# A limit of six loads in flight on one queue, and a warm-up cut into smaller products

## Chip, core and metric

The kernel runs on one core of a Trainium2 chip. The core has five engines that run side by side: TensorE (PE, matrix products; its weight loads are shown apart as PEld), VectorE (DVE), ScalarE (ACT), GpSimd (POOL) and SyncE (SP), which here only issues DMA transfers. Engines wait for one another, and for transfers, through semaphores. Sixteen DMA engines move data between the device memory (HBM) and the core's on-chip memory; a transfer is cut into pieces over all sixteen, and it has landed when the last of them is done.

The metric is the device time of one execution in microseconds (us), as a median over several runs.

## What is computed

The reference is an attention block without a softmax over keys, followed by a mixture-of-depths block. Shapes: 8 batches, 8 heads, 576 rows, head size 64; model width 512, hidden width 1024, capacity 128.

```python
q_s = exp(q - max(q, -1));  q_s /= sum(q_s, -1)      # over the head's 64 columns
k_s = exp(k - max(k, 2));   k_s /= sum(k_s, 2)       # over the 576 rows
kv  = einsum('bhsd,bhse->bhde', k_s, v)              # 64 x 64 for each head
x   = einsum('bhsd,bhde->bhse', q_s, kv)             # then heads side by side: B, S, 512

scores = einsum('bsd,d->bs', x, w_gate)
out = x.copy()
for b in range(B):
    top = the 128 rows of batch b with the largest scores
    h   = maximum(x[b, top] @ w1, 0)
    out[b, top] = x[b, top] + sigmoid(scores[b, top])[:, None] * (h @ w2)
```

## The kernel before, in words

Work is cut into 16 units; a unit is four heads of one batch, so two units make a batch. The program is written with a manual schedule: each engine runs its instructions in the order in which the code emits them, and an instruction that waits holds up everything behind it on its own engine.

For a unit, the loads bring k, v and q in two transfers each: for k and v one of 256 KB and one of 320 KB, for q two of 288 KB (three late units, 11, 13 and 15, take their q in four transfers of 144 KB with another layout, line 122). ACT takes the exponential of k (`k_exp`, line 249) and of q (`q_exp`, line 257); v is copied into a tile with a column of ones (`v_copy`, `v_copy_part`, lines 275 and 280, on DVE, POOL or ACT); TensorE forms kv (`kv_mm`, line 311, or `kv_mm_parts`, line 299, for unit 1), transposes q (`q_t`, lines 340 and 347) and multiplies the two (`x_mm`, line 375); DVE scales the result (`x_scale`, line 393), and SyncE stores it in two transfers (`x_store`, line 404). From the second unit of a batch on, scores are ranked (`compare`, line 443), the 128 best rows are gathered from the output by POOL (`fetch`, line 493), run through the two weight matrices (line 555 and line 564 for single batches, lines 648 and 704 for pairs of batches), and scattered back (line 573). The gathers read rows that the stores have written, so they wait for those stores.

Each of q, k and v has three buffers (`LD = 3`), so a load for unit u also waits until the buffer's user of unit u - 3 is done.

All loads are issued by SyncE, except one half of unit 0's k and the row of gate weights, which ACT issues. The function `load` (line 112) holds the issue calls for k, v and q, `load_w1` (line 154) four transfers of 512 KB, and `load_w2` (line 161) two of 1024 KB. The order at the start is: k, v, q of unit 0; q, k, v of unit 1; k of unit 2; then, behind a memset that DVE runs for the buffer, v and q of unit 2; w1; unit 3; unit 4; w2. The first stores, of unit 2, come after w2. Units 0 and 1 are stored much later (line 1104). After the start, each unit brings six loads and two stores in turn.

TensorE's first instructions are a warm-up: 12 products of 512 columns of ones (line 174), whose result nobody reads. Behind them come four products that spread the gate weights over partitions (line 860), one filler product (`fill`, line 854), and then kv of unit 0 (line 311), which needs the exponential of k from ACT and the copy of v from DVE.

`general` (line 777) is a fallback for inputs outside a range that the program checks at its end. It issues loads through the same functions and is not run for these inputs.

Of the kernel before, what the change touches and what calls it, by code (L numbers as in the profile page):

```python
# [17 lines left out]
def kernel(  # L18
# [23 lines left out]
    nc = tc.nc  # L42
    B, H, S, D = q.shape
    DM, F = moe_w1.shape
    P = 128
    R = 5
    N2 = R - 1
    T = R + N2
# [4 lines left out]
    SD = S * D  # L53
# [7 lines left out]
    NV = 5  # L61
    TURNED = frozenset((11, 13, 15))
    HC = 32
    WARM = 12
    assert S == 64 * T and D == 64 and DM == H * D and DM == 512 and H % 4 == 0
    assert 1 < capacity < S and KF == 8 and NQ == 2
    assert B * S <= 32 * 256
# [14 lines left out]
    def bank(tag, bufs):  # L82
        return ps.tile([P, 512], F32, tag=tag, name=tag, bufs=bufs)
# [9 lines left out]
    def place(b):  # L93
        return (b - 1) % B
# [4 lines left out]
    def rows_of(b, upward):  # L99
# [4 lines left out]


    LD = 3
    raw = {w: [const.tile([P, 2, T, D] if w == "q" else [P, 4, R, D], F32, name=f"{w}{n}") for n in range(LD)]
           for w in "qkv"}

    by_vector = TURNED  # L110

    def load(u, which, queues=(nc.sync, nc.sync)):
        b, qd = units[u]
        for what in which:
            src = {"q": q, "k": k, "v": v}[what]
            t = raw[what][u % LD]
            first = src[place(b), 4 * qd].offset
            if what == "q" and u in by_vector:

                for g in range(4):  # L120
                    i, c = divmod(g, 2)
                    nc.sync.dma_start(
                        out=t.rearrange("p h r d -> p (h r d)")[HC * g:HC * (g + 1)],
                        in_=bass.AP(tensor=src.tensor, offset=first + 2 * i * SD + HC * c,
                                    ap=[[T * D, HC], [D, T], [SD // 2, 4], [1, HC]]))
                continue
            if what == "q":
                for h in range(2):
                    queues[h].dma_start(out=t[:, h].rearrange("p r d -> p (r d)"),
                                        in_=bass.AP(tensor=src.tensor, offset=first + 2 * h * SD,  # L130
                                                    ap=[[T * D, P], [1, T * D]]))
                continue
            for n, rows in ((1, N2), (0, R)):
                queues[n].dma_start(
                    out=t[n::2, :, :rows].rearrange("p h r d -> p h (r d)"),
                    in_=bass.AP(tensor=src.tensor, offset=first + n * R * D,
                                ap=[[T * D, 64], [SD, 4], [1, rows * D]]))

    ctx.enter_context(tc.manual_schedule())
    for what in "kv":  # L140
# [7 lines left out]
                                               ap=[[DM, 1], [1, DM]]))  # L148
    w1 = const.tile([P, KD, F], F32, name="w1")
    w2 = const.tile([P, KF, DM], F32, name="w2")  # L150
# [3 lines left out]
    def load_w1(half):  # L154

        c = slice(half * F // 2, (half + 1) * F // 2)
        for d in range(0, KD, 2):
            nc.sync.dma_start(out=w1[:, d:d + 2, c],
                              in_=moe_w1[d * P:(d + 2) * P, c].rearrange("(d p) f -> p d f", p=P))

    def load_w2(n):
        half = KF // 2
        nc.sync.dma_start(out=w2[:, n * half:(n + 1) * half],
                          in_=moe_w2[n * half * P:(n + 1) * half * P].rearrange("(f p) d -> p f d", p=P))

    ones_b = const.tile([P, 4 * P], BF16, name="ones_b")
    nc.vector.memset(ones_b, 1.0)
    w_ps = bank("tp", 2)  # L170
    ones_f = const.tile([1, D], F32, name="ones_f")
    nc.vector.memset(ones_f, 1.0)
    for n in range(WARM):
        nc.tensor.matmul(out=w_ps, lhsT=ones_b[:, :P], rhs=ones_b, start=True, stop=True)
    warm = const.tile([P, 1], F32, name="warm")
    nc.scalar.activation(out=warm, in_=ones_b[:, :1], func=AF.Exp)
    ident = const.tile([P, P], F32, name="ident")
# [20 lines left out]
    for n in range(2):  # L198
        t = const.tile([P, 2, C], F32, name=f"kv_w{n}")
# [47 lines left out]
    def k_exp(u):  # L247
        ke = at.tile([P, 4, R, D], F32, tag="ke", name="ke", bufs=1)
        nc.scalar.activation(out=ke, in_=raw["k"][u % LD], func=AF.Exp)  # L249
        st["ke", u] = ke  # L250

    def q_exp(u, c):
        if c == 0:
            st["qe", u] = at.tile([P, T, 2, D], F32, tag="qe", name="qe", bufs=1)
        r0, r1 = ROWS[c]
        qr = raw["q"][u % LD].rearrange("p i r d -> p r i d")
        nc.scalar.activation(out=st["qe", u][:, r0:r1], in_=qr[:, r0:r1], func=AF.Exp)  # L257

    def q_exp_turned(u):
        qe = st["qe", u] = at.tile([P, T, 2, D], F32, tag="qe", name="qe", bufs=1)  # L260
        nc.scalar.activation(out=qe.rearrange("p r a t -> p (r a t)"),
                             in_=raw["q"][u % LD].rearrange("p h r d -> p (h r d)"), func=AF.Exp)

# [9 lines left out]
    def v_copy(u, engine=nc.vector):  # L273
        copy = engine.copy if engine is nc.scalar else engine.tensor_copy
        copy(out=v_ones[:, :, :, :D], in_=raw["v"][u % LD])  # L275

# [25 lines left out]
    def kv_mm(u, pairs=range(2)):  # L302

        ke, vo = st["ke", u], v_ones
        if 0 in pairs:
            st["kv", u] = bank("tp", 2)[:, :2 * (D + 1)].rearrange("p (i c) -> p i c", i=2)
        kv = st["kv", u]
        for i in pairs:
            for r in range(R):
                for h in range(2):  # L310
                    nc.tensor.matmul(out=kv[part(h), i], lhsT=ke[:, 2 * h + i, r], rhs=vo[:, 2 * h + i, r],  # L311
                                     start=(r == 0), stop=(r == N2))

    def kv_out(u):

        qd = units[u][1]
        kv = st.pop(("kv", u))
        kw = kv_w[u % 2]
        nc.vector.reciprocal(out=krec[:, u], in_=kv[:, :, D])
        nc.vector.tensor_mul(kw[:, :, :D], kv[:, :, :D], krec[:, u].to_broadcast([P, 2, D]))  # L320
        prod = at.tile([P, 2, D], F32, tag="prod", name="prod")
        for i in range(2):
            nc.vector.scalar_tensor_tensor(prod[:, i], kv[:, i, :D], krec[:, u, i:i + 1], wg[:, qd, i],
                                           op0=OP.mult, op1=OP.mult, accum_out=kw[:, i, D + 1:])
# [29 lines left out]
    def x_mm(u, a, wide=False):  # L354


        qT = st["qT", u] if a == 0 else st.pop(("qT", u))
        x = st["x", u, a] = ps.tile([P, 2, 512], F32, tag="x", name="x", bufs=2)
        kw = kv_w[u % 2]
        for r in range(R):  # L360
            for i, c in QUARTERS:
                if r == N2 and c:

                    nc.tensor.matmul(out=x[part(c), i, r * C:(r + 1) * C], lhsT=ones_b[part(i), :D],
                                     rhs=ones_b[part(i), :C], start=True, stop=True)
                    continue
                if wide and c:
                    continue
                both = wide and r < N2
                to = x[:, i] if both else x[part(c), i]  # L370
                if u in by_vector:
                    lhsT = qT[part(i), R * c + r, a]
                else:
                    lhsT = qT[part(i), a, r].rearrange("p c t -> p (c t)") if both else qT[part(i), a, r, c]
                nc.tensor.matmul(out=to[:, r * C:(r + 1) * C], lhsT=lhsT, rhs=kw[part(i), a], start=True, stop=True)  # L375
# [20 lines left out]
    def x_out(u):  # L396
        x_sums(u)
        x_scale(u, 0)
        x_scale(u, 1)
# [375 lines left out]
        nc.vector.tensor_sub(t, t, qm.to_broadcast([P, 2 * T, D]))  # L775

    def general():
        nonlocal by_vector
        by_vector = frozenset()
        for half in range(2):  # L780
            load_w1(half)
            load_w2(half)
        for b in range(B):
            for u in (NQ * b, NQ * b + 1):
                load(u, "kvq")
                shift(u)
                k_exp(u)
                q_exp(u, 0)
                q_exp(u, 1)
                v_copy(u)  # L790
                kv_mm(u)
                kv_out(u)
                q_t(u, 0)
                q_t(u, 1)
                for i in range(2):
                    x_mm(u, i)
                x_out(u)
                x_store(u)
            score(b, 0)
            score_parts(b)  # L800
            score_row(b, 1.0)
            for r in range(R):
                compare_exact(b, r)
            for step in (hits, find, fetch, gate, gated, turn):
                step(b)
            for f in range(KF):
                mlp1(b, f)
            for f in range(KF):
                mlp2(b, f)
            finish(b)  # L810
# [48 lines left out]
    for h in range(2):  # L859
        nc.tensor.matmul(out=g_ps[part(h), :4 * D], lhsT=ones_f,  # L860
                         rhs=w_row.rearrange("o (n i x) -> o i n x", i=2, x=2 * D)[:, h], start=True, stop=True)
# [11 lines left out]
    q_t(0, 1)  # L873
    load(2, "vq")
    load_w1(0)
    load_w1(1)
    q_exp(1, 0)
    q_exp(1, 1)
# [123 lines left out]
    for s in range(FIRST, SETTLED):  # L1002
        odd = s % 2 == 1
        here = s // 2 if odd else s // 2 - 1
        first = s == FIRST + 1
# [200 lines left out]
```

## Time and profile before

| what | us |
|---|---|
| median of 3 runs | 196.93 |
| the three runs | 196.46, 196.93, 198.37 |
| the profiled execution | 197.7 |
| its span, first to last instruction | 195.8 |
| TensorE busy in the span | 184.2 |

The profile is of one execution, which took 197.7 us; the span of its own instructions is 195.8 us, and the remaining 1.9 us lie around it. Times in the views count from the start of the span. A row of the chain of waits has a start, a length and what was under way; the time order of an engine has a start, a length, the engine (with a q where it is only its sequencer that issues a transfer), the line, the operation, the tiles as out<-in, and how many were merged into the row; brackets hold the idle time before it and what ended it.

### The profile page before, as it was taken

The page shows a single profiled execution, that of the slowest core. Times are in us where ns is not written, and L with a number is a line of the kernel's source. Part 1 is how long each engine was busy: PE and PEld are TensorE (multiplying, and loading weights), DVE is VectorE, ACT ScalarE, POOL GpSimd, SP SyncE. Part 2 cuts the span into 40 slices and gives each one's busy share as a digit, 9 for nine tenths or more (in the row PEclk, how much of TensorE's full clock was granted, in tenths as well). Part 3 has the DMA queues.
Part 4 walks back from the last instruction along what each step waited for, and adds up shares of the span by engine and source line. Part 5 has one row for each costly group of instructions (what it writes and reads, how often), then busy time and mean ns, then how long its engine had stood idle before and what let it go on. Part 6 is the DMA issues. An engine that isn't in the chain of part 4 may idle for free.

```text
span 195.8 us, 7049 instructions
## 1 busy us (share of the span) xinstructions
PE 184.2 (94%) x2927; PEld 156.0 (80%) x2927; DVE 130.4 (67%) x429; ACT 99.7 (51%) x160; POOL 72.7 (37%) x131
## 2 busy tenths in 40 slices
PE   5798899999999999999999999999999999999990
PEld 2466699894679996769999888899998889898860
DVE  6377966494669749928978989489959955444010
ACT  3474625658199759938675759365423133312100
POOL 8013551100860392099682312242314354701230
PEclk9999999999999999999999999999999999999997
DMA  5999999999999999989999799989451514010011
GB/s 153 364 365 378 378 368 364 328 388 352 341 379 374 336 314 363 308 248 152 312 325 320 130 317 330 273 160 257 158 121 57 121 38 149 32 54 5 3 56 63
DMA packets 48361, 46.67 MB, mean 238 GB/s; under 512 B 16321, under 2 KB 41921, under 8 KB 48322
## 3 DMA queue, kind: packets, MB, share of 16 engines
q1 hardware_dynamic: 46768, 41.62, 67.4%
q0 software_dynamic: 1280, 4.20, 6.7%
q8 instruction: 25, 0.41, 0.9%
q10 hardware_dynamic: 274, 0.33, 0.5%
q14 instruction: 14, 0.11, 0.2%
HBM read 34.61 MB, written 11.53 MB: 236 GB/s over the span
## 4 chain that ended last, share of the span: by engine, by line
PE 85%; DVE 6%; DMA 3%; issue 1%; ACT 1%; POOL 1%; POOLq 0%; DVEq 0%
PE mm L704 19%; PE mm L648 18%; PE tp L311 10%; PE x L375 10%; PE mm L555 8%; PE mm L564 8%; PE x L347 4%; DMA v<-in_v_dram 3%; PE mm L509 2%; PE tp L432 2%; PE x L530 2%; DVE xs L393 1%; DVE v_ones L280 0%; PE tp L468 0%; DVE v_ones L275 0%
## 5 line engine op out<-in xcount | busy, mean ns | idle before, releaser
L443 DVE SCALAR_TENSOR_TENSOR junk<-srow,s,stairs 128x576 bf16<-128x576 f32 x40 | 33.4, 834 | 1.5 <-ACT srow L435 0.8
L393 DVE TENSOR_TENSOR xs<-x,qrec 128x640 f32<-128x640 f32 x32 | 25.2, 815 | 0.0
L375 PE MATMUL x<-kv_w,qT 64*64 64x66 f32 x1152 | 23.2, 222 | 1.2 <-issue 0.5
L375 PEld LDWEIGHTS x<-kv_w,qT 64*64 64x64 f32 x1152 | 20.7, 134 | 4.5 <-issue 2.1
L352 ACT COPY qT<-x 128x512 f32<-128x512 f32 (+1 forms) x24 | 14.3, 643 | 17.1 <-PE x L347 16.6
L311 PE MATMUL tp<-v_ones,ke 128*64 128x65 f32 x600 | 21.6, 224 | 1.4 <-DVE v_ones L275 1.1
L704 PE MATMUL mm<-w,hT 128*128 128x256 f32 x96 | 22.2, 379 | 0.0
L249 ACT ACTIVATE ke<-k 128x1280 f32<-128x1280 f32 x16 | 20.4, 1274 | 3.4 <-issue 1.4
L311 PEld LDWEIGHTS tp<-v_ones,ke 128*64 128x64 f32 x600 | 19.2, 137 | 3.6 <-issue 1.9
L493 POOL DMA_INDIRECT xr<-out_dram,idx x8 | 8.1, 1018 | 36.3 <-DVE no L486 9.8
L704 PEld LDWEIGHTS mm<-w,hT 128*128 128x128 f32 x96 | 17.8, 190 | 2.2
L257 ACT ACTIVATE qe<-q 128x640 f32<-128x640 f32 (+1 forms) x26 | 16.4, 683 | 5.7 <-DMA q<-in_q_dram 3.0
L704 PE MATMUL mm<-tw,hT 128*128 128x256 f32 (+1 forms) x80 | 17.6, 363 | 0.0
L648 PE MATMUL mm<-xT,w 128*128 128x128 f32 x144 | 17.5, 276 | 0.0
L275 ACT COPY v_ones<-v 128x1280 f32<-128x1280 f32 x12 | 15.1, 1258 | 3.8 <-PE tp L311 2.5
L648 PEld LDWEIGHTS mm<-xT,w 128*128 128x128 f32 x144 | 16.8, 192 | 0.1
L555 PE MATMUL mm<-xT,w 128*128 128x128 f32 x128 | 16.7, 281 | 0.0
L713 POOL TENSOR_TENSOR o<-o,xr 128x256 f32<-128x256 f32 x9 | 6.8, 757 | 23.6 <-ACT o L712 23.6
L564 PE MATMUL mm<-w,hT 128*128 128x512 f32 x32 | 15.6, 611 | 0.0
L555 PEld LDWEIGHTS mm<-xT,w 128*128 128x128 f32 x128 | 15.0, 191 | 0.5
L704 PEld LDWEIGHTS mm<-tw,hT 128*128 128x128 f32 x80 | 13.8, 190 | 2.0 <-DVE o L717 0.4
L386 DVE RECIPROCAL qrec<-x 128x10 f32<-128x10 f32 x32 | 7.0, 217 | 12.6 <-PE x L375 12.2
(162 smaller groups left out, 311.2 us busy)
## 6 DMA issues: line engine op xcount, KB each, us to landing
q<-in_q_dram SPq DMA_DIRECT2D x26, 288.0 KB, 5.7
v<-in_v_dram SPq DMA_DIRECT2D x16, 320.0 KB, 5.4
out_dram<-xs SPq DMA_DIRECT2D x16, 320.0 KB, 5.6
k<-in_k_dram SPq DMA_DIRECT2D x15, 320.0 KB
k<-in_k_dram SPq DMA_DIRECT2D x16, 256.0 KB, 5.9
v<-in_v_dram SPq DMA_DIRECT2D x16, 256.0 KB
out_dram<-xs SPq DMA_DIRECT2D x16, 256.0 KB, 4.8
w<-in_moe_w_dram SPq DMA_DIRECT2D x4, 512.0 KB, 8.2
```

The source lines that it names most:

```text
L249: nc.scalar.activation(out=ke, in_=raw["k"][u % LD], func=AF.Exp)
L257: nc.scalar.activation(out=st["qe", u][:, r0:r1], in_=qr[:, r0:r1], func=AF.Exp)
L275: copy(out=v_ones[:, :, :, :D], in_=raw["v"][u % LD])
L311: nc.tensor.matmul(out=kv[part(h), i], lhsT=ke[:, 2 * h + i, r], rhs=vo[:, 2 * h + i, r], start=(r == 0), stop=(r == N2))
L352: nc.scalar.copy(out=to, in_=src)
L375: nc.tensor.matmul(out=to[:, r * C:(r + 1) * C], lhsT=lhsT, rhs=kw[part(i), a], start=True, stop=True)
L393: nc.vector.tensor_mul(xs[b][:, :, qd, :, a].rearrange("p r i d -> p i r d"), x[:, :, :, :D], rec.to_broadcast([P, 2, R, D]))
L443: nc.vector.scalar_tensor_tensor(junk, st["srow", b], st["s", b][:, r:r + 1], not_before[r], op0=OP.subtract, op1=OP.is_ge, accum_out=st[" ...
L555: nc.tensor.matmul(out=h_ps[:, f % HT * m:(f % HT + 1) * m], lhsT=w1[:, d, f * P:(f + 1) * P], rhs=xT[:, d, :m], start=(d == 0), stop=(d = ...
L564: nc.tensor.matmul(out=st["y", b][:m], lhsT=st["hT", b][:, f // HT, f % HT, :m], rhs=w2[:, f], start=(f == 0), stop=(f == KF - 1))
L648: nc.tensor.matmul(out=out_ps[:, f * m:(f + 1) * m], lhsT=w[:, k, f * P:(f + 1) * P], rhs=x()[:, k], start=first and f == 0 and k == 0, st ...
L704: nc.tensor.matmul(out=ps_of[to][:m, c:c + step], lhsT=st["hT", a][:, n, f, :m], rhs=w[:, f, c:c + step], start=first and f == 0, stop=f = ...
```

## The change

Two things are changed. A function `paced` is put around every issue of a load of q, k, v, w1 and w2. It keeps the names of the loads in the order of issue, and from the seventh on it makes each wait until the load six places ahead has landed. Stores and the gate weights are not counted and get no wait. ACT's half of unit 0's k is counted, as the second load. In the fallback the list is switched off.

The warm-up has 22 products of 280 columns in place of 12 of 512.

```diff
-    WARM = 12
+    WARM = 22
...
     LD = 3
+    AHEAD = 6
+    transfers = []
+
+    def paced(inst):
+
+        ins = inst.ins
+        if transfers is not None:
+            transfers.append(ins.name)
+            if len(transfers) > AHEAD:
+                tc.add_manual_dep(ins, transfers[-1 - AHEAD], mybir.DependencyInfo(
+                    mybir.DependencyClass.Sync, mybir.DependencyReason.DATA))
...
             for n, rows in ((1, N2), (0, R)):
-                queues[n].dma_start(
+                paced(queues[n].dma_start(
                     out=t[n::2, :, :rows].rearrange("p h r d -> p h (r d)"),
                     in_=bass.AP(tensor=src.tensor, offset=first + n * R * D,
-                                ap=[[T * D, 64], [SD, 4], [1, rows * D]]))
+                                ap=[[T * D, 64], [SD, 4], [1, rows * D]])))
...
     for n in range(WARM):
-        nc.tensor.matmul(out=w_ps, lhsT=ones_b[:, :P], rhs=ones_b, start=True, stop=True)
+        nc.tensor.matmul(out=w_ps[:, :280], lhsT=ones_b[:, :P], rhs=ones_b[:, :280], start=True, stop=True)
...
     def general():
-        nonlocal by_vector
+        nonlocal by_vector, transfers
         by_vector = frozenset()
+        transfers = None
```

The calls for q (both layouts), w1 and w2 are wrapped in the same way as that for k and v.

More of the change, by code (lines that the diff above doesn't have):

```diff
@@ L121, in load @@
                     i, c = divmod(g, 2)
-                    nc.sync.dma_start(
+                    paced(nc.sync.dma_start(
                         out=t.rearrange("p h r d -> p (h r d)")[HC * g:HC * (g + 1)],
                         in_=bass.AP(tensor=src.tensor, offset=first + 2 * i * SD + HC * c,
-                                    ap=[[T * D, HC], [D, T], [SD // 2, 4], [1, HC]]))
+                                    ap=[[T * D, HC], [D, T], [SD // 2, 4], [1, HC]])))
                 continue
@@ L128, in load @@
                 for h in range(2):
-                    queues[h].dma_start(out=t[:, h].rearrange("p r d -> p (r d)"),
-                                        in_=bass.AP(tensor=src.tensor, offset=first + 2 * h * SD,
-                                                    ap=[[T * D, P], [1, T * D]]))
+                    paced(queues[h].dma_start(out=t[:, h].rearrange("p r d -> p (r d)"),
+                                              in_=bass.AP(tensor=src.tensor, offset=first + 2 * h * SD,
+                                                          ap=[[T * D, P], [1, T * D]])))
                 continue
             for n, rows in ((1, N2), (0, R)):
-                queues[n].dma_start(
+                paced(queues[n].dma_start(
                     out=t[n::2, :, :rows].rearrange("p h r d -> p h (r d)"),
                     in_=bass.AP(tensor=src.tensor, offset=first + n * R * D,
-                                ap=[[T * D, 64], [SD, 4], [1, rows * D]]))
+                                ap=[[T * D, 64], [SD, 4], [1, rows * D]])))
     ctx.enter_context(tc.manual_schedule())
@@ L157, in load_w1 @@
         for d in range(0, KD, 2):
-            nc.sync.dma_start(out=w1[:, d:d + 2, c],
-                              in_=moe_w1[d * P:(d + 2) * P, c].rearrange("(d p) f -> p d f", p=P))
+            paced(nc.sync.dma_start(out=w1[:, d:d + 2, c],
+                                    in_=moe_w1[d * P:(d + 2) * P, c].rearrange("(d p) f -> p d f", p=P)))
     def load_w2(n):
         half = KF // 2
-        nc.sync.dma_start(out=w2[:, n * half:(n + 1) * half],
-                          in_=moe_w2[n * half * P:(n + 1) * half * P].rearrange("(f p) d -> p f d", p=P))
+        paced(nc.sync.dma_start(out=w2[:, n * half:(n + 1) * half],
+                                in_=moe_w2[n * half * P:(n + 1) * half * P].rearrange("(f p) d -> p f d", p=P)))
     ones_b = const.tile([P, 4 * P], BF16, name="ones_b")
```

## The prediction

> **What bounds the kernel now.** I read the page first, then the engines' busy time by stretches, the chain of waits, and last SyncE's own order of time.
>
> ```profile
> span 195.8 us, 7049 instructions
> PE 184.2 (94%) x2927; PEld 156.0 (80%) x2927; DVE 130.4 (67%) x429; ACT 99.7 (51%) x160; POOL 72.7 (37%) x131
> ...
> DMA  5999999999999999989999799989451514010011
> ...
> 8.50:24.00 15.50, 13.36 (x328) 10.75 (x329) 11.62 (x39) 9.71 (x15) 4.91 (x12) 1.00 1.06 375
> 24.00:190.00 166.00, 165.02 (x2581) 143.44 (x2581) 113.89 (x363) 87.20 (x142) 63.16 (x105) 1.00 0.75 232
> ```
>
> The first three lines are the page, the last two the stretches (length, then the busy time of PE, weight load, DVE, ACT and POOL, the clock, the DMA share and GB/s). From 24 to 190 us TensorE is busy for 165.02 of 166.00 us: later than that, a load that lands sooner brings nothing, and one that lands later costs nothing until its slack is used up. Time can move in the first 24 us, where TensorE idles for 15.50 - 13.36 = 2.14 us after 8.50, and before that. In the same time the DMA engines are full, at 375 GB/s, and stay so for most of the first half of the span.
>
> ```profile
> 2.32 5.13 DMA v<-in_v_dram
> ...
> 13.32 0.47 DVE xs L393
> ...
> 13.97 0.97 DVE v_ones L280
> ...
> 18.02 0.73 POOL v_ones L280
> ...
> 18.80 0.80 PE tp L311 x20
> ```
>
> This is the head of the chain of waits (start, length, what). Unit 0 starts when the second half of its v lands, at 2.32 + 5.13 = 7.45 us. Unit 1's v is copied at 13.97, behind DVE's own work. Unit 2's v is copied by POOL at 18.02, and the products on it start at 18.80. So three v loads pace the head, and each comes out of a full DMA queue.
>
> **What the waits do.** I number the loads in the order in which they are issued. 1 to 4 are k and v of unit 0 (2 is ACT's), 5 and 6 its q, 7 to 12 q, k, v of unit 1, 13 to 18 k, v, q of unit 2, 19 to 22 w1, 23 to 34 units 3 and 4, 35 and 36 w2. After these come two stores, and from there on each unit has six loads and two stores.
>
> ```profile
> 2.97 2.04 SPq L129 DMA_DIRECT2D q<-in_q_dram  x4
> ...
> 6.84 1.33 SPq L134 DMA_DIRECT2D v<-in_v_dram  x2
> 8.21 1.34 SPq L134 DMA_DIRECT2D k<-in_k_dram  x2
> ...
> 14.05 2.90 SPq L158 DMA_DIRECT2D w<-in_moe_w_dram  x4
> ...
> 20.72 2.25 SPq L129 DMA_DIRECT2D q<-in_q_dram  x2
> ...
> 14.53 0.47 SPq L158 DMA_DIRECT2D w<-in_moe_w_dram  x1
> DMA to landing us min/median/max: 7.5/7.5/7.5
> 22.02 0.94 SPq L129 DMA_DIRECT2D q<-in_q_dram  x1
> ```
>
> The last three lines show a limit that is there already. Load 20 is issued at 14.53 and takes 7.5 us: it lands at 22.0. Load 28, the eighth after it, is issued at 22.02. SyncE thus already waits for the landing of the eighth transfer ahead. The change tightens eight to six, and only in loads 7 to 36: once a unit brings two stores, the sixth load ahead is the eighth transfer ahead, and the new wait falls on the old one.
>
> In the head it binds almost every load. Three examples, with the time to landing from the same view of one instruction at a time:
>
> ```profile
> DMA to landing us min/median/max: 5.2/5.2/5.2
> ...
> DMA to landing us min/median/max: 6.3/6.3/6.3
> ...
> DMA to landing us min/median/max: 8.9/8.9/8.9
> ```
>
> Load 11, issued at 6.84, will wait for load 5 (2.97 + 5.2 = 8.2): 1.3 us later. Load 19 (14.05) waits for load 13 (8.21 + 6.3 = 14.5): 0.5 us. Load 27 (20.72) waits for load 21, the third w1 piece, issued at 15.04, 8.9 us: 23.9, so 3.2 us later. The issue moves by 0.5 to 3.2 us. What counts is whether the landing moves.
>
> ```profile
> 8.00:14.00 6.00, 5.14 (x143) 4.00 (x143) 3.73 (x14) 3.86 (x6) 0.12 (x1) 1.00 1.06 371
> ...
> q<-in_q_dram SPq DMA_DIRECT2D x26, 288.0 KB, 5.7
> ...
> DMA to landing us min/median/max: 3.8/3.8/3.8
> ...
> DMA to landing us min/median/max: 4.6/5.0/6.6
> ```
>
> Rows: the rate in the head; the size of a load (k and v pair 256 and 320 KB, so 288 is also their mean); the last 256 KB store at 152 us, with only its twin beside it; the loads of line 134 from 55 to 85 us, under full traffic. At 371 GB/s a mean load (294,912 B) occupies the engines for 0.795 us. Six in flight are 4.77 us of work, eight are 6.36, about the 6.3 of the second example. So today's time to landing is nearly all queue. When a load lands, five are left: 3.97 us of work. A new transfer with nothing ahead lands 3.8 us after its issue, of which 262,144 B / 371 GB/s = 0.71 is its own data: it needs 3.1 us of cover and has 3.97. The DMA engines then never run dry, the order of the loads is the same, and the landings stay where they are. Price of the wait: from below 0 (a landing cannot come sooner than its bytes, apart from rival two), from above rival one. I take 0, because 3.8 is the row with the same queue, size class and direction of issue, and it leaves 0.9 us to spare.
>
> [...]
>
> What is queued behind, and what the waits cost SyncE:
>
> ```profile
> 43.23 2.36 SPq L134 DMA_DIRECT2D k<-in_k_dram  x2
> ...
> 48.44 1.27 SPq L134 DMA_DIRECT2D k<-in_k_dram  x2
> ...
> 49.45 1.17 POOL L493 DMA_INDIRECT xr<-out_dram,idx  x1 [9.71 <-DMA out_dram<-xs]
> ...
> L134 SPq EVENT_SEMAPHORE  x8: 17/17/17, 56.2 to 79.9; - x8
> ```
>
> Behind the waits stand, on SyncE, the w2 loads 35 and 36, then the stores of unit 2. They slip by about 1 us. The stores are next asked for by a gather of POOL, at 49.45 us, which waits for the later stores of unit 3, so nobody is late for them. After 36 only loads 49 to 52 come close: 49 (48.44) is issued 5.2 us after 43 (43.23), with no store between, so it may wait up to the 6.3 - 5.2 = 1.1 us by which a loaded transfer outlasts that; these loads feed unit 7, while TensorE works on units 4 and 5. A wait costs SyncE 17 ns (the row of line 134), and SyncE has idle time for a hundred of them. POOL and ACT issue no load that is moved: load 2 is ACT's and too early to wait. The fallback `general` switches the waits off and is not run.
>
> **The warm-up.**
>
> ```profile
> 2.07 4.45 PE L174 MATMUL tp<-ones_b 128*128 128x512 bf16 x12 [2.07 <-DVE second_p L182]
> 6.45 0.65 PE L860 MATMUL tp<-w_row,ones_f 1*64 1x256 f32 x4
> 7.03 0.39 PE L854 MATMUL mm<-ones_b 128*128 128x512 bf16 x1
> 8.51 0.30 PE L311 MATMUL tp<-v_ones,ke 128*64 128x65 f32 x3 [1.09 <-DVE v_ones L275]
> ...
> 5.04 0.15 PEld L174 LDWEIGHTS <-ones_b 128*128 128x128 bf16 x1 [0.28 <-issue]
> 5.46 0.56 PEld L174 LDWEIGHTS <-ones_b 128*128 128x128 bf16 x3 [0.27 <-issue]
> ...
> 29.23 0.28 PE L477 MATMUL tp<-vals,hit 128*128 128x5 bf16 x5
> ```
>
> Columns: 12 x 512 = 6144, 22 x 280 = 6160. Products start 0.43 us apart up to 5.46, then about twice as fast: the clock doubles there. A slow product of 280 columns takes 0.43 x 280 / 512 = 0.235 us, so 14.4 run by 5.46, and 7.6 more at half of that take 0.9: the end is at 6.4, where it is now (6.52 with the drain). For what ten more products cost beside their columns, the bounds are 0 and 0.056 us each (five products of 5 columns in 0.28): 0 to 0.56 in all. I take 0.1, nearer to 0, since a stream of columns hides the start of the next. Either way it is covered: behind the warm-up come lines 860 and 854, and then TensorE idles 1.09 us for v. If that cover were gone, the 0.1 would be late at line 311. Twenty more instructions also shift the places at which TensorE's code is loaded; the idle pieces called "issue" are at most 0.4 us each, so ±0.4 at most, and I take 0.
>
> **Sum**, against the profiled execution: 197.7 us (span 195.8 and 1.9 around it); waits 0, warm-up 0 (hidden), so 197.7. The median of the three runs, 196.93, is 0.8 below that execution; the forecast for a median is 196.9.
>
> **Rivals.**
>
> One, slower: the engines run dry. Place: loads 7 to 36. If a load's round trip under traffic is longer than 4.77 us, each load comes (trip - 4.77) / 6 late on top of the one before. For: single loads of the 55 to 85 us row take 6.6. Against: its smallest is 4.6, and the longer ones stand in a queue. At 5.6, midway between the two, that is 0.14 us a load. Unit 2's v is 10 loads in: 1.4 us late, 0.2 of it covered by TensorE's products on unit 1. Unit 3's v is 20 loads in, 2.8 late; its slack shows in two rows:
>
> ```profile
> 28.71 1.26 POOL L275 COPY v_ones<-v 128x1280 f32<-128x1280 f32 x1 [1.91 <-DMA v<-in_v_dram]
> 31.33 1.39 PE L311 MATMUL tp<-v_ones,ke 128*64 128x65 f32 x40
> 43.82 1.88 PE L564 MATMUL mm<-w,hT 128*128 128x512 f32 x4
> DMA to landing us min/median/max: 10.7/10.7/10.7
> ```
>
> The copy ends at 29.97, 1.4 us before its products; with the 1.2 that TensorE has already lost that leaves another 0.2. w2 (second piece issued at 30.19, 10.7 to landing: 40.9) has 2.9 us until line 564 and costs nothing. Total +1.4: 198.3. At 6.6 it is 0.305 a load and +4.8: 201.7. It decides from a trip of 4.77 on, and passes 1% at about 5.9.
>
> Two, faster: fewer transfers in the queues let the early ones land sooner. For: v of unit 0 takes 5.13 us for the fourth load. Against: the first wait stands at load 7, behind it, and unit 1's v copy starts no sooner than DVE ends its work at 13.79 (0.18 before), and unit 2's products start no sooner than 0.2 before 18.80. So about 0.4: 196.5. Its ceiling is all the idle time of the head, 2.14 + 1.09 = 3.2 us: 193.7.
>
> Three, the clock: 280-column products do not raise it at 5.46. If it comes one such stretch later (3.4 us, to 8.9), lines 860 and 854 take twice 1.0 us, which the 1.09 us of idle covers, and line 311 starts slow for 0.4 us: +0.4, 197.3. Staying slow through the head would double 13.36 us; nothing speaks for that, since the products follow each other without a gap as before.
>
> **How the numbers follow.** Forecast 0.72, rival one 0.14, two 0.10, three 0.04. A measurement of this kernel can tell about 1% (2 us) from no change. Over 1% slower is the upper part of rival one (trip above 5.9) and the worst of three: 0.09. Over 1% faster is the far part of rival two: 0.06. Within 1%: 0.85. The range runs from 195.9 (rival two with the runs' own 0.5 us below the median) to 198.6 (rival one at 5.6, and a little over); outside are the far ends of one and two.
>
> **What would show it.** Right: SyncE's loads 7 to 36 start 0.5 to 3 us later, take under 5 us to landing instead of 6, the DMA share of the head stays at 1.06 and 375 GB/s, unit 0's v lands near 7.4, POOL's copy for unit 2 starts near 18.0, and line 174 ends near 6.5. Wrong: a DMA share below 1 between 8 and 32 us with POOL's copy after 19 (rival one); unit 0's v landing before 7 (rival two); weight loads of line 174 still 0.23 us apart after 6 us (rival three).

## The result, and the profile after

| kernel | median us | lowest to highest | ratio to before [95%] |
|---|---|---|---|
| before, same chip | 197.32 (6 runs) | 196.46 to 200.77 | |
| changed | 200.37 (6 runs) | 198.9 to 203.06 | 1.0113 [1.0066, 1.016] |

The change makes the kernel 1.1% slower; the forecast was no change, 196.9 us with a range up to 198.6. Ratios here and below compare undisturbed runs only, medians and means are over all runs of a kernel, so the two can differ by half a per cent. The profiled execution took 200.6 us.

The page of the changed kernel, with the rows that answer to those of before. Lines of the code stand 12 further down than before (the load is line 146 instead of 134).

```profile
span 198.7 us, 7070 instructions
PE 184.9 (93%) x2937; PEld 157.1 (79%) x2937; DVE 130.1 (65%) x429; ACT 100.1 (50%) x160; POOL 76.8 (39%) x131
PEclk9999999999999997999999999999999999999997
DMA  4999999999999899979899999979752504110011
```

The span is 2.9 us longer, TensorE's busy time only 0.7. Apart from the last slice, which stands at 7 in both, the clock row has one slice below full speed, the 16th (74.5 to 79.5 us), which before did not have. The DMA row is too coarse for what follows: a nine is any share of 90% or more, and full engines show 1.06 in the finer rows.

The chain of waits of the changed kernel, its middle part (start, length, what was under way):

```profile
22.68 5.71 DMA v<-in_v_dram
28.41 5.59 DMA v<-in_v_dram
34.00 10.44 DMA k<-in_k_dram
44.53 1.50 SPq L146
47.64 5.51 DMA v<-in_v_dram
53.17 6.72 DMA v<-in_v_dram
61.83 6.96 DMA out_dram<-xs
69.61 5.47 DMA xr<-out_dram,idx
76.82 4.19 PE mm L576 x6
```

From 22.68 to 75 us this chain is loads and stores on SyncE, one after another, and it comes out at one transfer: the gather of batch 2's rows, landing at 69.61 + 5.47 = 75.08. TensorE's order of time there, first before, then changed:

```profile
73.13 0.71 PE L432 MATMUL tp<-ident,s_all 128*128 128x128 f32 x5
73.77 0.63 PE L530 MATMUL x<-ident,xr 128*128 128x128 f32 x4
```

```profile
72.48 0.71 PE L444 MATMUL tp<-ident,s_all 128*128 128x128 f32 x5
75.22 0.63 PE L542 MATMUL x<-ident,xr 128*128 128x128 f32 x4 [2.03 <-DMA xr<-out_dram,idx]
76.61 4.40 PE L576 MATMUL mm<-w,hT 128*128 128x512 f32 x6
```

Up to the row at 72.48 the changed kernel is 0.65 us ahead. Then the transposes of the gathered rows (`turn`, line 542) wait 2.03 us: 1.45 us behind. Of the products at 76.61, most run at half clock. The same stretch and the earlier one in which the loads are slow, as busy time (length; PE, weight load, DVE, ACT, POOL; clock, DMA share, GB/s), before and changed:

```profile
26.00:32.00 6.00, 6.00 (x137) 5.69 (x137) 3.43 (x15) 3.01 (x4) 1.81 (x3) 1.00 1.06 366
74.00:80.00 6.00, 6.00 (x87) 4.15 (x88) 5.61 (x13) 6.00 (x11) 0.58 (x3) 1.00 1.04 352
```

```profile
8.00:14.00 6.00, 5.63 (x146) 4.31 (x147) 3.73 (x14) 4.36 (x7) 0.53 (x1) 1.00 1.06 362
26.00:32.00 6.00, 6.00 (x137) 5.69 (x137) 3.20 (x13) 3.01 (x4) 1.55 (x2) 1.00 0.96 318
74.00:80.00 6.00, 4.78 (x17) 2.79 (x18) 3.81 (x9) 4.01 (x6) 5.14 (x9) 0.72 1.00 336
```

Between 26 and 32 us the DMA share falls from 1.06 to 0.96 and the rate from 366 to 318 GB/s. Between 74 and 80 the clock is 0.72: one window of 3.41 us at half speed, from 76.53 to 79.94 by the clock records, which costs some 1.7 us, half of its length. So the loss of this execution has two terms: 0.65 + 1.45 = 2.1 us at the gather, and 1.7 by the clock, together 3.8. The 0.65 had been won before, and some 0.4 is won back near 140 us, which leaves 2.8 of the 2.9.

The gather starts late because it waits for the stores of unit 5; POOL's rows for it, before and changed:

```profile
66.93 1.00 POOL L493 DMA_INDIRECT xr<-out_dram,idx  x1 [8.70 <-DVE krec L319]
```

```profile
69.61 1.01 POOL L505 DMA_INDIRECT xr<-out_dram,idx  x1 [9.88 <-DMA out_dram<-xs]
```

Before, POOL waited for DVE; now it waits for a store. That store was issued at 61.83 instead of 59.84 and landed at 68.79 instead of 65.56 us. By the landing records fifteen of its sixteen pieces were there at 67.33 and the last came 1.46 us later (before: 0.29). A 16 KB transfer of the instruction queue, begun at 65.26, took 2.22 us, where the others of this execution took 0.9 to 1.5. This is where theory B of the first expectations comes from. It cannot be the rule: in E6 and E16 below no such transfer from 45 to 70 us took over 1.1 us, and their gathers landed later still.

### The profile page after: what moved, and what is told of

Read it like the earlier page. It is cut to its first block, busy times and chain, and to the rows that moved or that the text cites. A ratio compares the mean times of both kernels' runs of the same rounds, so it can differ in the third digit from the quotient of the medians.

```text
span 198.7 us, 7070 instructions
## 1 busy us (share of the span) xinstructions
PE 184.9 (93%) x2937; PEld 157.1 (79%) x2937; DVE 130.1 (65%) x429; ACT 100.1 (50%) x160; POOL 76.8 (39%) x131
## 3 DMA queue, kind: packets, MB, share of 16 engines
q0 software_dynamic: 1280, 4.20, 6.4%
## 4 chain that ended last, share of the span: by engine, by line
PE 56%; DMA 34%; DVE 3%; SPq 2%; issue 1%; POOLq 0%; ACT 0%; POOL 0%; DVEq 0%
PE mm L716 18%; PE mm L660 18%; DMA v<-in_v_dram 12%; DMA k<-in_k_dram 10%; PE tp L323 5%; PE x L387 5%; PE mm L576 4%; DMA out_dram<-xs 4%; DMA w<-in_moe_w_dram 3%; DMA xr<-out_dram,idx 3%; DMA q<-in_q_dram 2%; SPq L146 2%; PE x L359 2%; PE x L542 2%; PE tp L444 1%
## 5 line engine op out<-in xcount | busy, mean ns | idle before, releaser
L387 PE MATMUL x<-kv_w,qT 64*64 64x66 f32 x1152 | 22.7, 222 | 0.6 <-DVE qT L362 0.3
L323 PE MATMUL tp<-v_ones,ke 128*64 128x65 f32 x600 | 21.0, 224 | 1.8 <-DVE v_ones L287 0.9
L576 PE MATMUL mm<-w,hT 128*128 128x512 f32 x32 | 17.5, 670 | 0.1
```

The source lines that it names most:

```text
L576: nc.tensor.matmul(out=st["y", b][:m], lhsT=st["hT", b][:, f // HT, f % HT, :m], rhs=w2[:, f], start=(f == 0), stop=(f == KF - 1))
```

## The experiments

The first expectations name their theories by letters. C is the one that the chain above suggests: the waits on loads 7 to 36 leave the DMA engines short of work, w2 and all behind it land later, and the backlog reaches the gather. D: the waits from load 37 on do it. Where another letter stands, its sentence says what it holds.

### One part alone

E1 is the kernel before with the new warm-up (its diff below), E2 the changed kernel with the same lines put back.

```diff
-    WARM = 12
+    WARM = 22
-        nc.tensor.matmul(out=w_ps, lhsT=ones_b[:, :P], rhs=ones_b, start=True, stop=True)
+        nc.tensor.matmul(out=w_ps[:, :280], lhsT=ones_b[:, :P], rhs=ones_b[:, :280], start=True, stop=True)
```

E1, the warm-up alone:

> Only the warm-up is changed (22 products of 280 columns); no load waits for another. Theory A (the waits make the stores of unit 5 land late, the gather of batch 2 behind them lands after TensorE asks for it, TensorE stalls 2.0 us and its clock then halves for 3.4 us): same as before within 0.5 us, no wait of TensorE on the gather, its first load of batch 2's rows near 73.5 us. Theory B (20 more TensorE instructions move the loads of its code, and one of them, 2.2 us long at 65.3 us, holds up the stores): slower by 2 to 3 us, with the gather's stall.

E2, the waits alone:

> Only the waits; the warm-up stays 12 products of 512 columns. Theory A: slower by 2 to 3 us as the changed kernel, with a TensorE wait on the gather of 1.5 to 2.5 us near 74 us. Theory B: same as before within 0.5 us, no such wait.

E1: 1.0001 [0.9966, 1.0035]. E2: 0.9994 [0.9952, 1.0036]; its median is 199.06 against 198.56, 0.5 us more. Neither part alone is slower by anything that can be told, so neither theory A nor theory B holds as it was put: A wanted E2 slower with a wait on the gather, B wanted E1 slower. Yet E2's gather landed at 75.70, later than the changed kernel's 75.08. TensorE did not wait for it, because it came late itself: its order of time in E2 has

```profile
60.41 0.81 PE L323 MATMUL tp<-v_ones,ke 128*64 128x65 f32 x20 [0.85 <-issue]
```

an idle piece in which it waited for nothing that the profile shows, and more of them at 25.4 and 84.3 us, and a half clock early on, from 8.88 us. So the late gather comes with the waits, but its price depends on the rest.

### Which waits

On the old warm-up: E3 has the waits on loads 7 to 18 only (below), E5 on 7 to 36 (36 for 18 in the same line), E4 from 37 on (`len(transfers) > 36`).

```diff
-            if len(transfers) > AHEAD:
+            if AHEAD < len(transfers) <= 18:
```

> The waits stand on loads 7 to 18 alone (units 1 and 2), warm-up as before. If the 0.5 us by which unit 0's v landed sooner in the changed kernel comes from the waits, v lands near 7.0 and TensorE runs 0.3 to 0.5 us ahead from there on: 0.2 to 0.7 us faster than before. If it was chance, the same as before. In both cases no wait on the gather, since w1 and all behind it are loaded as before.

> The waits stand on loads 7 to 36 and not behind them, warm-up as before. Theory C (the engines run short between 26 and 34 us, w2 lands 1.3 us late, and the backlog carries this to the stores of unit 5): w2 lands near 42.3, the gather's stall is there with 1 us or more, 1.5 to 3 us slower. Theory D (the waits on loads 49 to 58 hold SyncE and the stores behind them; the head does no harm): as before within 0.5 us, no stall.

> The waits stand on load 37 and all behind it, none on 7 to 36; warm-up as before. Theory C (the engines run short under the waits on 19 to 36, and the backlog carries it on): w2 lands near 41 and the gather of batch 2 near 73.2, as before; time as before within 0.5 us. Theory D (the waits on loads 49 to 58 hold the stores back): the gather lands 1 to 2 us later than in before, near 75.

E3: 1.0002 [0.9963, 1.0041], gather at 73.19, 371 GB/s between 26 and 32 us. E5: 0.9985 [0.9931, 1.004], gather at 75.18, 338 GB/s. E4: 1.0006 [0.9952, 1.006], gather at 72.38. So D falls. In these three profiles the waits on loads 7 to 36 delay the gather by 2 us and those on 7 to 18 do not, without making these kernels measurably slower. That it is the waits on 19 to 36 does not follow yet: between 8 and 14 us, where only the waits on 7 to 18 can act, E5's rate was 321 GB/s and E3's 369. In E5 TensorE again lost time of its own at the same place as in E2:

```profile
59.25 0.81 PE L323 MATMUL tp<-v_ones,ke 128*64 128x65 f32 x20 [1.09 <-issue]
```

### The changed kernel again, and its stores earlier

E6 is the changed kernel once more. E7 is the changed kernel with k and v of unit 8 issued behind the stores of unit 5, not ahead of them, so that the gather's stores come sooner; E8 is the same move with the new warm-up and no waits.

```diff
-        if s in HEAD:
+        if s in HEAD and s != 5:
             load(s + 3, "kv")
...
-        load(s + 3, "q" if s in HEAD else "kvq")
+        load(s + 3, "q" if s in HEAD and s != 5 else "kvq")
```

> The changed kernel itself once more, beside the others and in as many executions as they. Waits alone and the warm-up alone each measured the same as before (0.9994 and 1.0001 of it). Theory A (the waits put the gather of batch 2 two us late; with the new warm-up TensorE comes to it on time, idles about 2 us and then loses 1.7 us at half clock, while with the old warm-up a late code load of 0.8 to 1.1 us holds TensorE back already and hides a part): median 1 to 2 us above that of before, and the profile has the gather landing near 75 us. Theory E (the first 1.13% was mostly the spread of six executions): median within 0.7 us of before.

> The changed kernel, with k and v of unit 8 loaded behind the stores of unit 5 and not ahead of them. Theory A (the late stores of unit 5 are what the gather waits for): the stores land about 3 us sooner, the gather of batch 2 lands at 72 to 73, TensorE does not wait for it, and the time comes down by 1 to 3 us against the changed kernel. If something else holds the gather (its index, POOL), it lands near 75 as in the changed kernel and nothing is gained.

> No waits, the new warm-up, and the same move of unit 8's k and v behind the stores of unit 5. Theory A: the gather lands 1 us or more before TensorE asks for it, where before it had 0.6 us to spare; 0.3 to 1 us faster than before in the median, since executions in which a code load or a full queue makes the gather late no longer pay. If the gather is late in no execution of before, the same as with the new warm-up alone.

E6: 1.018 [1.0126, 1.0234], with the wait at the gather again, 2.83 us, and a half clock from 76.31 to 79.72:

```profile
77.03 1.09 PE L542 MATMUL x<-ident,xr 128*128 128x128 f32 x4 [2.83 <-DMA xr<-out_dram,idx]
```

E7: 1.0107 [1.0055, 1.0159]. Its gather landed at 74.36 and TensorE did not wait for it, but it waited 0.90 us for VectorE at 65.88 and 0.57 us for ScalarE's copy of v at 71.63, and lost 1.36 us without a visible cause at 78.99. E8: 1.01 [1.0042, 1.0157], so the move itself costs 1%, and its gather landed at 75.43, not sooner. This pair was a miss: it says nothing on the gather's worth.

### How deep, and which waits with the new warm-up

E10 is the changed kernel with eight for six. E12 has waits on loads 7 to 18 only (the line of E3), E15 on 19 and later only (`len(transfers) > 18`); all three have the new warm-up.

```diff
-    AHEAD = 6
+    AHEAD = 8
```

> The changed kernel with each load waiting for the eighth load ahead of it instead of the sixth, warm-up 22 x 280. If it is six in flight that keeps the DMA engines from their full rate between 26 and 34 us: with eight the rate is back near 365 GB/s, batch 2's gather lands by 73.5 us, TensorE does not wait for it, and the time is 0.996 to 1.004 of before. If waits as such (their place in the queue, not their depth) are what costs: gather at 75 us or later, TensorE idle 2 us, 1.010 to 1.018.

> Waits on transfers 7 to 18 alone, with the new warm-up of 22 x 280. If the cost comes from the waits on transfers 19 to 36 (engines short of work between 26 and 34 us): batch 2's gather lands at 72.5 to 73.5 us, no wait on it, and 0.995 to 1.002 of before. If any of the waits together with the new warm-up costs: gather near 75 us, 1.010 or more.

> The changed kernel with the waits on transfers 19 and later alone, warm-up 22 x 280: the part that e12 left out. If the waits on 19 to 36 keep the engines short of work between 26 and 34 us: batch 2's gather lands at 74.5 us or later, TensorE waits 1 us or more, and the time is 1.008 to 1.018 of before. If the first waits (7 to 18) are needed for the loss: gather near 73 us and 0.996 to 1.004.

E10: 1.0049 [1.0013, 1.0086]; gather at 72.79, no wait on it. E12: 1.0034 [0.9993, 1.0075]; gather at 74.30, no wait, in an execution that had lost 1.7 us to the clock before. E15: 1.0211 [1.0158, 1.0264]. The busy time of the stretch in which the loads were slow, E10, then E15:

```profile
26.00:32.00 6.00, 6.00 (x124) 5.69 (x124) 3.31 (x14) 2.91 (x4) 1.69 (x3) 1.00 1.07 371
```

```profile
26.00:32.00 6.00, 6.00 (x115) 5.81 (x115) 1.91 (x12) 1.89 (x3) 1.60 (x3) 0.87 0.91 289
```

With eight in flight the engines are full (1.07); with six, from load 19 on, the share is 0.91. By the times it is thus the depth, and the later part of loads 7 to 36. E10's 0.5% above before is half of the changed kernel's loss at most, and is left without a cause. E15's time came out even above what was expected, its gather did not come as expected: it landed at 73.26 in the profiled execution, and TensorE, which had lost time to a half clock from 24.14 to 27.55 us, did not wait:

```profile
PEclk9999979999999999999999999999999999999997
```

That execution, 198.96 us, was the fastest of E15's six; the others took 201.02 to 203.33, and no profile shows one of them. So the path from the waits on 19 to 36 to E15's 2% is not shown, and E12's gather, with the other waits alone, was later than E15's. What holds over all profiles with the stores in their old place is the whole: the gather landed at 72.11 to 73.19 us in before, E1, E3, E4, E10 and E14, and at 75.08 to 77.54 in seven of the eight profiles that have six ahead on loads 7 to 36 (E13, the eighth, 73.59).

### Why only with the new warm-up

E11 keeps 22 products and 6160 columns, but makes them 512 and 48 columns in turn.

```diff
     for n in range(WARM):
+        wide = 512 if n % 2 == 0 else 48
-        nc.tensor.matmul(out=w_ps[:, :280], lhsT=ones_b[:, :P], rhs=ones_b[:, :280], start=True, stop=True)
+        nc.tensor.matmul(out=w_ps[:, :wide], lhsT=ones_b[:, :P], rhs=ones_b[:, :wide], start=True, stop=True)
```

> The changed kernel with a warm-up of 22 products of 512 and 48 columns in turn (11 of each): 6160 columns as in 22 x 280, and the same count of instructions, but another shape. If the two parts work together because 20 more instructions move the places at which TensorE waits for its code: as the changed kernel, 1.010 to 1.018 of before, with a wait on batch 2's gather of 2 us or more and a half clock behind it. If the evenness or length of the products (the clock at the start) is what matters: as with the waits and the old warm-up, 0.995 to 1.004.

E11: 1.0183 [1.0112, 1.0254], like the changed kernel. So the even length of 280 columns is not needed; what the two warm-ups share is 22 instructions instead of 12. The profiled execution lost its time in another way than was expected, though, with two half clocks early on and no wait on the gather (landed 76.48, TensorE still later):

```profile
PEclk9969979999999999999999999999999999999998
```

### Filling the idle time

E9 puts ten products of 512 columns, read by nobody, ahead of the transposes that wait.

```diff
+        for _ in range(10 if b == 2 and not alone else 0):
+            nc.tensor.matmul(out=both[:, 1], lhsT=ones_b[:, :P], rhs=ones_b, start=True, stop=True)
         for d in range(KD):
             nc.tensor.transpose(out=t_ps[:, d * m:(d + 1) * m], in_=xr[:m, d * P:(d + 1) * P],
```

> The changed kernel, with ten products of 512 columns of ones put on TensorE ahead of the transposes of batch 2's gathered rows, where the changed kernel idled 2.03 and 2.83 us; their results go to the unused half of the tile and are read by nobody. If the late gather idles TensorE and the idle time halves its clock: the products fill about 2.1 us, the wait on the gather is under 1 us, no half clock between 74 and 82 us, and the time is 1 to 2 us below the changed kernel's (about 1.003 to 1.010 of before). If the half clock has another cause: it stays near 76 us for 3.4 us, and the time stays at 1.011 to 1.018 of before or goes above it.

E9: 1.011 [1.0047, 1.0174], median 200.72, so the expected gain of 1 to 2 us did not come. The page's clock row and TensorE's order of time:

```profile
PEclk9999999999999999999999999999999999999999
```

```profile
73.83 2.33 PE L543 MATMUL x<-ones_b 128*128 128x512 bf16 x10
77.59 0.66 PE L545 MATMUL x<-ident,xr 128*128 128x128 f32 x4 [1.43 <-DMA xr<-out_dram,idx]
```

The gather landed at 77.54 here; TensorE was idle for 1.43 us instead of 3.6, and no half clock followed, which fits the idle time as its cause. Why the time did not fall with it is not shown; the filler holds TensorE for its 2.3 us also where the gather is less late.

### The gather off TensorE's path

E13 moves the four transposes, and ScalarE's sum over their result, to the end of their step, some 4 us later; nothing needs them before 92 us. E14 is the same move without waits, E16 the changed kernel beside them.

```diff
-            if on:
+            if on and s != SETTLED:
                 turn(ends - 1)
...
                 pieces(3)
+                if s == SETTLED:
+                    turn(ends - 1)
+                    size(ends - 1)
```

> The changed kernel with the four transposes of batch 2's gathered rows (and the size sum on ScalarE that reads them) moved to the end of their step, some 5 us later on TensorE; nothing needs them before about 92 us. If the late gather is where the changed kernel loses its time: no wait on it any more, no half clock behind it, and a time within 0.5% of e14 and of before (0.996 to 1.005), 2 to 3 us below the changed kernel of this call. If the waits cost TensorE elsewhere, and the gather is only where it shows: the time stays at 1.010 or more.

> Only the warm-up of 22 x 280, no waits, with the same move of the transposes as e13: what the move does where the gather is not late. Both theories: as the warm-up alone, 0.996 to 1.003 of before.

> The changed kernel itself once more, beside e13 and e15 on one chip. Both theories: 1.010 to 1.018 of before; the wait on batch 2's gather 2 to 3 us, with or without a half clock behind it.

E16: 1.0138 [1.009, 1.0185], median 201.12. E13: 1.003 [0.9988, 1.0072], median 199.41. E14: 1.001 [0.9971, 1.0049], median 198.69; before 198.23. TensorE in E16, then in E13:

```profile
76.58 1.08 PE L542 MATMUL x<-ident,xr 128*128 128x128 f32 x4 [3.23 <-DMA xr<-out_dram,idx]
77.45 1.92 PE L567 MATMUL mm<-xT,w 128*128 128x128 f32 x8
```

```profile
72.95 1.06 PE L567 MATMUL mm<-xT,w 128*128 128x128 f32 x8
73.84 2.74 PE L576 MATMUL mm<-w,hT 128*128 128x512 f32 x6
76.42 0.60 PE L542 MATMUL x<-ident,xr 128*128 128x128 f32 x4
```

In E13 the transposes run at 76.42 and wait for nothing; the products behind them go first. (The gather landed at 73.59 in this execution, so in their old place, at about 73, they would have waited only 0.6 us: it is the timed runs that carry the verdict.) The intervals of E13 and E16 do not meet, and the move brings back 201.12 - 199.41 = 1.7 of the 201.12 - 198.23 = 2.9 us. E14, the same move without waits, costs nothing that can be told. The wait on the gather is thus where most of the loss arises, not only where it shows.

### All runs by clock

Every run has a span and a mean granted clock; span x (1 - clock) is what it lost to the clock. Means over all runs, less two that stand far out (457 us of before, 363 us of E11), in us:

| kernel | runs | clock loss | time without it |
|---|---|---|---|
| before (the runs beside E1 to E16) | 91 | 1.1 | 197.5 |
| changed (the first runs, E6, E16) | 18 | 2.5 | 198.7 |
| E1, new warm-up alone | 12 | 1.8 | 196.6 |
| E2 and E5, old warm-up, waits | 24 | 1.4 | 197.8 |
| E15, waits from 19 on, new warm-up | 6 | 3.3 | 198.4 |
| E11, uneven warm-up, waits | 5 | 2.9 | 198.7 |
| E9, filled | 6 | 0.9 | 199.5 |
| E13, transposes later | 12 | 1.4 | 198.1 |

The mean of a group is uncertain by 0.2 (before) to 0.8 (six runs). The changed kernel's loss is about half clock (1.4) and half other time (1.2), such as the wait on the gather. E9 takes away the clock part and adds to the other; E13 takes away most of the clock part and perhaps half of the other.

## Why the prediction was wrong, point by point

**Which loads are bound: right.** Loads from 37 on were taken as unchanged; E4 gives 1.0006. For 7 to 36 the issues moved as forecast (load 27 from 20.72 to 24.09; forecast 23.9).

**"The DMA engines then never run dry": wrong, and the first failed step.** The sum set 3.97 us of work, left when a load lands, against 3.1 us that a new one needs. It took sixteen engines for one. A load has landed when the last engine has done its piece (load 29 of before: sixteen landing records from 28.23 to 30.86 us, and it landed at 30.86), and the engines are not level: this is when the first and the last of the sixteen pieces of a load finished, from the landing records of the trace, for the loads that landed between 29 and 33 us.

```
kernel              mean spread us   example (first piece to last)
before              2.62             27.5 to 30.1
E10, eight ahead    2.56             27.5 to 30.1
E12, loads 7 to 18  2.66             27.5 to 30.1
changed             1.60             29.0 to 30.5
E6                  1.96             28.7 to 30.9
E15                 1.66             29.5 to 30.8
E16                 1.50             30.3 to 31.4
```

The engine that is first ends 2.6 us ahead of the last, so by the prediction's own sum it has only 3.97 - 2.6 = 1.4 us of work left at the landing, an estimate, and needs 3.1. That the engines run dry is seen in the DMA share, 0.96 instead of 1.06 between 26 and 32 us, and in the spread, 1.60 instead of 2.62, which fits leaders that idle until the others have caught up. The five loads that landed there bear it out: their first pieces finish 0.76 us apart before (26.75 to 29.79) and 1.00 apart in the changed kernel (26.91 to 30.90), their last pieces 0.77 and 0.73. With eight, 7 x 0.795 - 2.6 = 3.0 is left by the same estimate, just what is needed, and E10's engines are full (a share of 1.07). Early in the program (8 to 14 us) the spread before is 1.1 us, and six ahead leave 2.9, just under the 3.1, and executions fall on both sides: of the eleven profiles with the waits on loads 7 to 18 the changed kernel's first, E3 and E16 kept 359 to 369 GB/s there (before 371), the other eight fell to 291 to 332. So these waits starve the engines too, in most executions; yet E3 and E12, which have them alone, are not measurably slower.

A round trip over 4.77 us, which rival one needs, is neither borne out nor refuted: loads 28 to 31 landed 4.4 to 4.5 us after issue, but 32 and 33 took 5.7, and loads 31 to 33 of E6 6.0 to 6.1. The engines ran dry already between loads 28 and 31, where the round trip was under 4.77, so it was not the step that failed.

**"The landings stay where they are": right within 0.7 us to load 31, wrong after it.** Load 29 landed at 30.52 (before 30.86), w2's second piece at 42.26 (40.94). What the leaders missed between 26 and 30 us were bytes of later loads, so the lateness shows only there. Rival one's mechanism came, but not at the place that it named: neither unit 2's v was late here (POOL's copy at 17.75, before 18.02) nor unit 3's (its products at 31.32, before 31.33). In E6, the same kernel, that copy began at 18.79.

**"Nobody is late for them": wrong, and the second failed step.** The prediction followed the stores to their next gather, at 49.45 us, and stopped. The next gather but one, at 66.93, landed at 73.15 before, and TensorE asked for it at 73.77. With 0.6 us to spare it was the tightest of the gathers (the others had 1.1 us or more), and in the views of before it could be read. A backlog of 1.3 us on SyncE's queue (w2) stands against 1.9 us at that gather; that full engines carry the one on to the other is read from the chain, which runs through transfers alone.

**The warm-up at nothing: right alone, wrong together.** It ended at 6.2 (forecast 6.4), and E1 gives 1.0001:

```profile
2.08 4.13 PE L186 MATMUL tp<-ones_b 128*128 128x280 bf16 x22 [2.08 <-DVE second_p L194]
8.01 1.18 PE L323 MATMUL tp<-v_ones,ke 128*64 128x65 f32 x33 [0.91 <-DVE v_ones L287]
```

At full clock the products of 512 columns start 0.215 us apart (before) and those of 280 columns 0.119 (changed), which is 1% more per column, so the ten more products cost next to nothing beside their columns; the prediction took 0.1. Rival two's sign was there, unit 0's v at 6.95, not 7.45, but by luck: in E6 its last piece landed at 7.96. The two parts were priced one by one and added; their interaction was no term of the sum, and this is the third failed step. It was measured: 1.0001 and 0.9994 apart, 1.0113, 1.018 and 1.0138 together. How it works stays open. The term nearest to it is "Twenty more instructions also shift the places at which TensorE's code is loaded ... ±0.4 at most, and I take 0". The gap of 0.85 and 1.09 us in E2 and E5 falls before TensorE's instruction 1985 in both (products, weight loads and the instructions of its sequencer counted together), and E2's other two before 705 and 3009, that is 1280 ahead of it and 1024 behind it, both whole multiples of 256. The page of before lists 25 transfers of 16 KB on the instruction queue; the first 22 start, on average, 248 of TensorE's instruction records apart (from record 337 to 5548), and in the changed kernel 249 (336 to 5566), which agrees with code that is loaded by the count of its instructions but ties none of them to a gap. In the changed kernel, E6, E9 and E16 there is no such gap between 26 and 73 us. In E2 and E5, where TensorE is held up anyway, the late gather (75.70 and 75.18) cost nothing that can be told. E11 agrees with the count of instructions as the cause and rules out the even shape; that the count acts through these places is argued from a few profiles, not shown.

**The clock: not foreseen at this place.** Rival three looked at the start only. There its sign came in E6, where all 22 products start 0.23 us apart and end at 7.39; but with the old warm-up E3 and E5 have all 12 at the slow pace too (to 7.18 and 7.32), so it is not the new products. In the middle, after idle pieces of 2.03, 2.83 and 3.23 us the clock fell to half for one window of 3.41 us; E9, with 1.43, kept it. Each of the three, at half speed for 3.41 us, cost some 1.7 us more, half of it. The length of one idle piece does not decide it alone, though: 1.88 us at 109.05 in E14 was followed by no half clock, and 0.58 and 0.74 in E12, a microsecond apart, by one. In two traces the half clocks start whole multiples of 3.413 us apart: 76.53 and 195.99 in the changed kernel (35 times), 10.36, 27.42 and 198.09 in E11 (5 and 50 times). In the 3.4 us just ahead of its half clock TensorE was busy for 1.39 of 3.42 us in the changed kernel, 1.29 of 3.41 in E6, 0.18 of 3.41 in E16 and 2.10 of 3.42 in E12; 1.98 of 3.41 in E9 and 1.75 of 3.41 in E14 brought none, so this busy time alone does not tell them apart, and what does is not shown.

**Open.** Why the two parts cost only together; why E10 is 0.5% above before; why the kernels with 22 products lose more to the clock also where the gather is in time (E1 1.8, E12 2.6 against 1.1); and what remains of the loss in E13, 1.2 us by the medians and 0.3% by the ratio. Its profile shows one place, the next gather, which landed at 91.67 instead of 89.26 us, after TensorE was ready for it:

```profile
91.81 0.63 PE L542 MATMUL x<-ident,xr 128*128 128x128 f32 x4 [1.16 <-DMA xr<-out_dram,idx]
```

## What to carry to other kernels

A limit on transfers in flight must be priced for the engine that is furthest ahead: work in flight less the spread between the sixteen engines, against the fixed part of a round trip (here an estimated 3.97 - 2.6 = 1.4 us against 3.1). When a queue slips, follow it to the transfer with the least slack in the whole program (here 0.6 us), not to its next reader. And two changes that cost nothing alone (here 1.0001 and 0.9994) can cost together (1.0113); time them together and apart.

## What was not expected of the hardware

- The sixteen pieces of one 256 to 320 KB load finished 1.1 us apart at 8 to 14 us and 2.6 us apart at 26 to 33 us under full traffic (before).
- TensorE's clock halved after an idle time of 2.03 us, for 3.41 us (changed, 76.53 to 79.94), and the half clocks of the changed kernel's trace start 35 times 3.413 us apart, those of E11's 5 and 50 times.
- A kernel's runs spread over 3 to 6 us (before: 196.48 to 202.39 in one series); half-speed windows at changing places make up a part of it, and idle pieces of up to 1.9 us that no wait explains perhaps another, so that one profile of each kernel was not enough to see what the means show.
